# The first 560 columns of an output projection's weights come through GpSimd's queue in six loads of unequal row counts

## The chip, the core and the metric

The kernel runs on one core of a Trainium2 chip. The metric is the device time of one execution in microseconds (us); lower is better. The core has a matrix engine (TensorE, PE in the profile), a vector engine (VectorE, DVE), an activation engine (ScalarE, ACT), a general engine (GpSimd, POOL) and a synchronisation engine (SyncE, SP) that here does nothing but issue DMA transfers. The transfers of every queue are carried out by 16 DMA engines, each of which works through its own ring of packets; this text calls one of them a ring. A load is finished when all rings that had a share of it have reported.

## What is computed

One decode step of a layer with grouped-query attention over a cache, gated by a bilinear feed-forward block, for two sequences with one new token each:

```python
xn = layernorm(x)                                   # x: [2, 1, 448]
q  = xn @ wq                                        # 16 heads of 256
s  = softmax(q @ k_cache.T / 16) @ v_cache          # 8 kv heads, 4096 positions, 256 wide
s  = s @ wo                                         # wo: [4096, 448]
g  = silu((xn @ w_gate * (xn @ w_up)) @ w_down)     # inner width 1792
return x + s * g
```

All is float32. The two caches are 134 MB together, the weights the rest of some 159 MB that are read once.

## The kernel before

**Loads.** All large loads are issued by SP, in the order of `dma_side`: the gate and up weights `wgu` into the tile `low`, `wd` into `buf[1]`, `wq` into `buf[0]`, then the caches. The caches go by `N` = 16 steps (8 kv heads times 2 sequences). One transfer of 8 MB (lines 128 to 130) carries the values of step i and the keys of step i+2, 64 KB to each of the 128 partitions, into one of two buffers `buf[0]`, `buf[1]`; it is issued when the matmuls on the buffer's earlier contents are done (`sp.after(pe, "v", i - 2)`). At the end come the values of the last two steps (`vv`, line 133) and the output weights `wo` (lines 134 to 138).

**The output weights.** `wo` is laid out as 128 partitions by 32 blocks of `D` = 448 columns. It comes in six loads of 14, 9, 4, 3, 1 and 1 blocks (`ABREAST` and `DIRECT`), each with a semaphore of its own (`won`). The first three go into `low`, whose earlier contents, `wgu`, were last read some 20 us into the kernel; so they are issued directly behind `vv`, and the queue works on them as soon as it gets there. The last three go into the upper half of `buf[1]` (`late`), and wait until the matmuls on it are done.

**Compute.** PE does for each step i: `turn` (transposes of the exponentials, line 317), `scores` (keys, line 361), `values` (line 386) and `join` (line 394), with the row maxima, exponentials, sums and copies of the results on DVE and ACT. Seven rounds of a hardware loop (line 407) hold steps 0 to 13, two each. `scores(i)` waits for a copy of the query on POOL: `pool_side` ends in a loop of 16 copies (line 158), the i-th of which waits until `scores(i - 2)` is done. POOL has no other work after the first few us.

**The end.** PE goes through the six loads of `wo` in order (lines 437 to 452): a wait for the load's semaphore, and then its blocks, four matmuls to a block in the last three loads. DVE then multiplies by the gate and adds `x` (lines 295 and 298), and SP stores the result (line 140).

Of the kernel before, what the change touches and what calls it, by code (L numbers as in the profile page):

```python
# [8 lines left out]
B, D = 2, 448  # L9
# [15 lines left out]
WO = 4 * HKV  # L25
ABREAST = (14, 9, 4)
DIRECT = (3, 1, 1)


class Queue:  # L30
# [23 lines left out]
def program(nc, known, x, xo, wgu, wd, wq, kv, vv, wo, out):  # L54
    def sb(name, shape):
        return nc.alloc_sbuf_tensor(name, shape, F32).ap()

    def ps(name, shape):
        return nc.alloc_psum_tensor(name, shape, F32).ap()

    first = nc.alloc_semaphore("first")
    sems = {n: nc.alloc_semaphore(n) for n in (
        "x", "xg", "gu", "wd", "wq", "k0", "k1", "v14", "v15", "t0", "t1", "pt", "sr", "ob", "q", "m", "mx", "res")}
    won = [nc.alloc_semaphore(f"wo{i}") for i in range(len(ABREAST + DIRECT))]
    pe = Queue(nc, nc.tensor, "pe", known)
    dv = Queue(nc, nc.vector, "dv", known)
# [6 lines left out]
    low = sb("low", [128, 28 * FC])  # L73
# [5 lines left out]
    one = sb("one", [1, 1])  # L79
    xnT = sb("xnT", [128, NK, W])  # L80
    xg, gate, sig, r0, r1 = (sb(n, [128, SL]) for n in ("xg", "gate", "sig", "r0", "r1"))
    sel = sb("sel", [128, 2, 2])
    pick = sb("pick", [128, B, DUP])
    gs, hs = sb("gs", [128, 512]), sb("hs", [128, 512])
# [5 lines left out]
    m = sb("m", [128, 2])  # L90
    mx = sb("mx", [1, NT, W])
    p = sb("p", [128, 2, 512])
    su = sb("su", [128, 2])
    sr = sb("sr", [128, 128])
    r = [sb(f"r{i}i", [128, REP]) for i in range(2)]
    pT = sb("pT", [128, 2, BLK, 128])
    ob = sb("ob", [128, 512])
# [4 lines left out]
    pt = [ps(f"pt{i}", [128, NK, 128]) for i in range(2)]  # L102
# [4 lines left out]
    late = buf[1][:, ROW:]  # L107
    bounds = [0]
    for n in ABREAST + DIRECT:
        bounds.append(bounds[-1] + n)  # L110
    early = bounds[len(ABREAST)]

    def wo_step(i):
        return low[:, i * D:(i + 1) * D] if i < early else late[:, (i - early) * D:(i - early + 1) * D]

    def where(i):
        return divmod(i, B)

    def dma_side():
        e = nc.sync  # L120
        for lo, hi in zip(GU, GU[1:]):
            e.dma_start(low[:, lo:hi], wgu[:, lo:hi]).then_inc(sems["gu"], 16)
        e.dma_start(buf[1][:, :14 * D], wd).then_inc(sems["wd"], 16)
        e.dma_start(buf[0][:, :28 * 512], wq).then_inc(sems["wq"], 16)
        sp.after(pe, "y4")
        for h in range(2):
            e.dma_start(buf[1][:, h * ROW:(h + 1) * ROW], kv[0][:, h * ROW:(h + 1) * ROW]).then_inc(sems[f"k{h}"], 16)
        for i in range(N - 2):
            sp.after(pe, *(("q", 1) if i == 0 else ("s", 1) if i == 1 else ("v", i - 2)))
            e.dma_start(buf[i % 2], kv[1 + i]).then_inc(turns[i % 2], 16)  # L130
        sp.after(pe, "v", N - 4)
        for h in range(2):
            e.dma_start(buf[0][:, h * ROW:(h + 1) * ROW], vv[h]).then_inc(sems[f"v{N - 2 + h}"], 16)
        for n, lo, hi in zip(won, bounds, bounds[1:]):
            if lo == early:
                sp.after(pe, "v", N - 3)
            t = low[:, lo * D:hi * D] if hi <= early else late[:, (lo - early) * D:(hi - early) * D]
            e.dma_start(t, wo[:, lo * D:hi * D]).then_inc(n, 16)
        sp.after(dv, "res")
        e.dma_start(out, r1).then_inc(sems["res"], 16)  # L140
        e.wait_ge(sems["res"], 16)
        last = nc.alloc_semaphore("last")
        e.sem_clear(range(first.num, last.num + 1))

    def pool_side():
        e = nc.gpsimd
        po.ev(e.memset(ident, 0.0), "zero")
        po.after(po, "zero")
        po.ev(e.affine_select(out=ident, in_=ident, pattern=[[-1, 128]], compare_op=OP.not_equal, fill=1.0,
                              base=0, channel_multiplier=1), "ident")  # L150
        po.after(dv, "var")
        po.ev(e.tensor_tensor(rstd, st[:, 3:4], eh, op=OP.pow), "rstd")
        po.after(dv, "qT")
        for i in range(N):
            g, b = where(i)
            if i >= 2:
                po.after(pe, "s", i - 2)
            e.tensor_copy(qs[i % 2], qT[:, g, b, :, None, :].to_broadcast([128, 2, DUP, REP])).then_inc(sems["q"], 1)  # L158

    def act_side():  # L160
        e = nc.scalar
        e.dma_start(x2, x).then_inc(sems["x"], 16)
        ac.after(dv, "xg")
        e.dma_start(xg[0:128:DUP, :], xo).then_inc(sems["xg"], 16)
        ac.after(pe, "gu", 0)
        ac.ev(e.copy(gs[:, :FC], s[:, 0, :FC]), "g")
        ac.after(pe, "y4")
        ac.ev(e.copy(ys, o[:, :D]), "ys")
        ac.after(pe, "y")
        ac.ev(e.activation(sig, acc[:, :SL], AF.Sigmoid), "sig")  # L170
        for h in range(2):
            ac.after(pe, "q", h)
            ac.ev(e.copy(qr[h], s[:, h]), "qr", h)

        def exps(i):
            ac.after(dv, "neg", i)
            for h in range(2):
                ins = e.activation(p[:, h], s[:, h], AF.Exp, bias=m[:, 1:2], scale=1.0 / 16, accum_out=su[:, h:h + 1])  # L178
            ac.ev(ins, "exp", i)

        def half(i):
            ac.after(pe, "t", i, 1)
            e.copy(pT[:, 1], pt[1]).then_inc(sems["pt"], 1)  # L183

        exps(0)
        half(0)
        exps(1)
        for i in range(N):
            if i + 2 < N:
                exps(i + 2)  # L190
            ac.after(pe, "v", i)
            e.copy(ob, o).then_inc(sems["ob"], 1)  # L192
            if i + 1 < N:
                half(i + 1)
        ac.after(pe, "w4")
        ac.ev(e.copy(ys, o[:, :D]), "accs")
# [103 lines left out]
    def pe_side():  # L300
        e = nc.tensor
# [18 lines left out]
        def abreast(t, lhs, rhs, i, total):  # L320
            c = i % NT
            return e.matmul(t[W * c:W * (c + 1), :D], lhs, rhs, start=i < NT, stop=i >= total - NT)  # L322

        def spread(start, stop):
            for c in range(NT):
                ins = e.matmul(acc[W * c:W * (c + 1), :SL], pick.rearrange("p b j -> p (b j)"),  # L326
                               ys[:, c * SL:(c + 1) * SL], start=start, stop=stop)
            return ins
# [77 lines left out]
        at, count = dict(pe.at), pe.n  # L406
# [26 lines left out]
        def left(i):  # L433
            g, j = divmod(i, 4)
            return oT[g][:, j // 2, j % 2].rearrange("p b j -> p (b j)")

        for n, lo, hi in zip(won, bounds, bounds[1:]):
            e.wait_ge(n, 16)
            for i in range(lo, hi):
                if i >= 4 * (HKV - 1):  # L440
                    pe.after(dv, "oT", N - 1)
                if i < early:
                    ins = abreast(o, left(i), wo_step(i), i, early)
                else:
                    for c in range(NT):
                        ins = e.matmul(acc[W * c:W * (c + 1), :SL], left(i), wo_step(i)[:, c * SL:(c + 1) * SL],  # L446
                                       start=lo == early and i == lo, stop=i == WO - 1)
            if hi == early:
                pe.ev(ins, "w4")
            if lo == early:  # L450
                pe.after(ac, "accs")
                spread(False, False)
        pe.ev(ins, "fin")

    pool_side()
    act_side()
    dve_side()
    dma_side()
    pe_side()
    return {q.name: q.at for q in (pe, dv, ac, po, sp)}  # L460

# [44 lines left out]
```

## Time and profile before

| what | value |
|---|---|
| time, median of 3 runs | 374.98 us (374.97 to 375.02) |
| the profiled execution's own time | 375.17 us |
| its span, first to last instruction | 373.9 us |
| read from memory in the span | 158.54 MB, 424 GB/s |
| PE busy | 243.6 us, 65% of the span |
| DVE, ACT, POOL busy | 60.3 us, 45.7 us, 5.0 us |
| granted TensorE clock, mean | 0.794 |

The views used below are: the page's strip of the DMA engines' busy share in 40 slices; its list of DMA queues, where each row gives packets, megabytes, and the time that the packets took as a share of 16 rings' span; the chain of work that ended last; a table by stretches of time, whose last two columns are the mean busy share of the 16 rings and the rate; and the timeline of instructions. Queue q1 is SP's, q10 ACT's; "instruction" rows are the fetches of the engines' program code, which run on the same rings. In the table by stretches, a packet counts with its whole time in the stretch in which it starts, so that a share over a very short stretch is rough.

### The profile page before, as it was taken

Reading aid. Unit: us, or ns where it says so; the run is one execution under the profiler, and the core shown is the slowest. Engines: PE = TensorE matmul, PEld = TensorE weight load, DVE = VectorE, ACT = ScalarE, POOL = GpSimd, SP = SyncE. Lnnn points to the kernel's source line nnn. Section 1 sums busy time; section 2 is a strip of 40 time slices with the busy share of each in tenths; the row PEclk is TensorE's granted clock in tenths of the full one; section 3 lists DMA queues with packets and bytes.
Section 4 is the critical chain, followed back from the end, with each engine's and each line's share of the span. In section 5 each row is a group of like instructions: output and inputs, shape, how many; then the busy total and the mean of one; then the engine's idle time right before and its main releaser. Section 6 shows DMA issues by size and latency. Waiting matters only on the chain. (4 is left out here: it accounts for less than half of the span.)

```text
span 373.9 us, 3749 instructions
## 1 busy us (share of the span) xinstructions
PE 243.6 (65%) x1642; PEld 95.1 (25%) x1642; DVE 60.3 (16%) x142; ACT 45.7 (12%) x105; POOL 5.0 (1%) x23
## 2 busy tenths in 40 slices
PE   0093295739393948585776767575758484849786
PEld 0021022322322222323231313122322222232332
DVE  3001002202121212112021203030302020202100
ACT  1002021010102020202020202020202010201110
POOL 1000000000000000000000000000000000000000
PEclk9998588758677687768596859596959586958899
DMA  9999999999999999999999999999999999999995
GB/s 369 400 459 413 430 424 438 444 444 449 449 429 400 435 429 435 449 442 436 407 435 435 435 442 435 449 428 414 435 428 442 442 442 442 400 417 435 417 421 211
DMA packets 4203, 158.70 MB, mean 424 GB/s; under 512 B 610, under 2 KB 868, under 8 KB 1252
## 3 DMA queue, kind: packets, MB, share of 16 engines
q1 hardware_dynamic: 4176, 158.59, 98.4%
q8 instruction: 5, 0.08, 0.1%
q14 instruction: 2, 0.02, 0.0%
q10 hardware_dynamic: 20, 0.01, 0.0%
HBM read 158.54 MB, written 0.06 MB: 424 GB/s over the span
## 5 line engine op out<-in xcount | busy, mean ns | idle before, releaser
L361 PE MATMUL s<-buf,qs 128*32 128x512 f32 x512 | 89.2, 860 | 58.1 <-PEq L51 58.1
L386 PE MATMUL o<-buf,pT 128*32 128x512 f32 x512 | 76.9, 610 | 0.3 <-DVE oT L272 0.3
L178 ACT ACTIVATE p<-s,m 128x512 f32<-128x512 f32 x32 | 21.7, 682 | 251.6 <-DVE m L253 251.6
L361 PEld LDWEIGHTS s<-buf,qs 128*32 128x32 f32 x512 | 22.5, 151 | 111.2 <-issue 111.1
L247 DVE TENSOR_REDUCE m<-s 128x1 f32<-128x1024 f32 x16 | 19.6, 1224 | 144.8 <-PE s L361 144.8
L317 PE MATMUL pt<-ident,p 128*128 128x128 f32 x128 | 22.2, 329 | 12.8 <-PEq L51 12.8
L394 PE MATMUL oc<-sel,ob 128*128 128x2 f32 x128 | 16.4, 250 | 19.8 <-PEq L51 19.8
L386 PEld LDWEIGHTS o<-buf,pT 128*32 128x32 f32 x512 | 17.1, 111 | 32.9 <-issue 30.6
L394 PEld LDWEIGHTS oc<-sel,ob 128*128 128x128 f32 x128 | 15.5, 191 | 33.9 <-issue 33.9
L317 PEld LDWEIGHTS pt<-ident,p 128*128 128x128 f32 x128 | 17.4, 166 | 13.7 <-issue 13.7
L308 PE MATMUL s<-buf,xnT 128*32 128x512 f32 x48 | 7.9, 813 | 10.8 <-DMA buf<-wq 10.8
L308 PE MATMUL s<-low,xnT 128*32 128x448 f32 x48 | 6.5, 692 | 11.9 <-DMA low<-wgu 11.9
L266 DVE COPY pT<-pt 128x512 f32<-128x512 f32 x16 | 11.1, 691 | 18.3 <-PE o L386 17.0
L249 DVE TENSOR_REDUCE mx<-sm 1x128 f32<-1x512 f32 x16 | 10.9, 679 | 10.1 <-PE sm L367 10.1
L192 ACT COPY ob<-o 128x512 f32<-128x512 f32 x16 | 9.3, 582 | 12.5 <-PE o L386 12.5
L183 ACT COPY pT<-pt 128x512 f32<-128x512 f32 x16 | 9.6, 601 | 2.4 <-PE pt L317 2.4
L371 PEld LDWEIGHTS sm<-one,mx 1*128 1x128 f32 x32 | 4.7, 183 | 13.8 <-issue 13.8
L158 POOL COPY qs<-qT 128x64 f32<-128x64 f32 x16 | 3.7, 236 | 293.8 <-PE s L361 243.1
L377 PEld LDWEIGHTS sm<-sel,sr 128*128 128x128 f32 x32 | 7.4, 288 | 0.0
L371 PE MATMUL sm<-one,mx 1*128 1x1 f32 x32 | 6.0, 255 | 1.7 <-PEq L51 1.7
L322 PE MATMUL o<-low,oT 128*32 128x448 f32 x54 | 6.4, 544 | 0.6 <-DMA low<-wo 0.6
L178 ACT ACTIVATION_READ_ACCUMULATOR p<-s,m 128x1 f32 x32 | 6.3, 196 | 0.0
(65 smaller groups left out, 62.4 us busy)
## 6 DMA issues: line engine op xcount, KB each, us to landing
buf<-kv SPq DMA_DIRECT2D x2, 4096.0 KB, 26.1
buf<-vv SPq DMA_DIRECT2D x2, 4096.0 KB, 23.1
buf<-wq SPq DMA_DIRECT2D x1, 7168.0 KB, 41.9
low<-wgu SPq DMA_DIRECT2D x1, 5824.0 KB, 17.0
buf<-wd SPq DMA_DIRECT2D x1, 3136.0 KB, 24.0
low<-wo SPq DMA_DIRECT2D x1, 3136.0 KB, 34.8
low<-wo SPq DMA_DIRECT2D x1, 2016.0 KB, 39.1
low<-wo SPq DMA_DIRECT2D x1, 896.0 KB, 40.9
```

Of the source, the lines that this page charges most:

```text
L178: ins = e.activation(p[:, h], s[:, h], AF.Exp, bias=m[:, 1:2], scale=1.0 / 16, accum_out=su[:, h:h + 1])
L183: e.copy(pT[:, 1], pt[1]).then_inc(sems["pt"], 1)
L192: e.copy(ob, o).then_inc(sems["ob"], 1)
L247: e.tensor_reduce(m[:, 0:1], s.rearrange("p h n -> p (h n)"), axis=AX.X, op=OP.max).then_inc(sems["m"], 1)
L249: e.tensor_reduce(mx, sm[:1, None, :128].rearrange("p o (c j) -> p o j c", c=NT).to_broadcast([1, NT, W, NT]), axis=AX.X, op=OP.max).then_ ...
L266: e.tensor_copy(pT[:, 0], pt[0]).then_inc(sems["pt"], 1)
L308: e.matmul(t[W * c:W * (c + 1), :n], xnT[:, k, :], block(NT * k + c), start=k == 0, stop=False)
L317: ins = e.transpose(t[:, i, :], a[:, i * 128:(i + 1) * 128], ident)
L361: ins = e.matmul(s[W * c:W * (c + 1), h], qs[i % 2][:, d].rearrange("p j q -> p (j q)"), k[:, h, d, c, :], start=d == 0, stop=d == 1)
L371: pe.ev(e.matmul(sm[:, 128:129], mx.rearrange("p c j -> p (c j)"), one, start=True, stop=True), "x", i)
L386: ins = e.matmul(o[W * at:W * (at + 1), :], pT[:, h, j, 64 * c + 16:64 * c + 48], v[:, h, j, c, :], start=h == 0 and j < 2, stop=h == 1 an ...
L394: ins = e.matmul(oc[:, 2 * d:2 * d + 2], ob[:, h * 256 + d * 128:h * 256 + (d + 1) * 128], sel[:, h], start=h == 0, stop=h == 1)
```

## The change

Before the change each of SP's first three loads of `wo` brought all its columns. Now the first `LEAD` = 560 columns (2,240 bytes of each of the 128 partitions, 0.29 MB in all) are left out of SP's first load, and come through POOL's queue instead, early in the kernel: behind the fifth of its 16 copies (i = 4), POOL issues six loads. Five bring those columns, of 7, 34, 2, 51 and 34 rows, 128 together; between the fourth and the fifth of them stands one of a single row of 16 columns into an unused tile `skip`. The space was last read by the gate and up matmuls, so nothing has to be waited for. PE waits for the five loads (semaphore `lead`, 16 for each) before its first block of `wo`, and SP waits for the sixth (`skip`) before the store of the result.

```diff
+LEAD = D + D // 4
+SHARES = (7, 34, 2, 51, 0, 34)
...
         for n, lo, hi in zip(won, bounds, bounds[1:]):
             if lo == early:
                 sp.after(pe, "v", N - 3)
-            t = low[:, lo * D:hi * D] if hi <= early else late[:, (lo - early) * D:(hi - early) * D]
-            e.dma_start(t, wo[:, lo * D:hi * D]).then_inc(n, 16)
+            if hi <= early:
+                at = max(lo * D, LEAD)
+                e.dma_start(low[:, at:hi * D], wo[:, at:hi * D]).then_inc(n, 16)
+            else:
+                e.dma_start(late[:, (lo - early) * D:(hi - early) * D], wo[:, lo * D:hi * D]).then_inc(n, 16)
+        e.wait_ge(sems["skip"], 16)
         sp.after(dv, "res")
         e.dma_start(out, r1).then_inc(sems["res"], 16)
...
             e.tensor_copy(qs[i % 2], qT[:, g, b, :, None, :].to_broadcast([128, 2, DUP, REP])).then_inc(sems["q"], 1)
+            if i == 4:
+                row = 0
+                for n in SHARES:
+                    if n:
+                        e.dma_start(low[row:row + n, :LEAD], wo[row:row + n, :LEAD]).then_inc(sems["lead"], 16)
+                    else:
+                        e.dma_start(skip, wo[:1, :16]).then_inc(sems["skip"], 16)
+                    row += n
...
+        e.wait_ge(sems["lead"], 16 * sum(n > 0 for n in SHARES))
         for n, lo, hi in zip(won, bounds, bounds[1:]):
             e.wait_ge(n, 16)
```

On POOL, from the end of its short start to its last instruction, before the change (L158 is the copy of the query for one step):

```order
L147 MEMSET ident 128x128
L149 ISA
L149 AFFINE_SELECT ident<-ident 128x128
L152 TENSOR_TENSOR rstd<-st,eh 2x1
L158 COPY qs<-qT 128x64 x16
```

and in the changed kernel, where the copy is L165:

```order
L159 TENSOR_TENSOR rstd<-st,eh 2x1
L165 COPY qs<-qT 128x64 x5
L170 DMA low<-wo 7x560
L170 DMA low<-wo 34x560
L170 DMA low<-wo 2x560
L170 DMA low<-wo 51x560
L172 DMA skip<-wo 1x16x1
L170 DMA low<-wo 34x560
L165 COPY qs<-qT 128x64 x11
```

Six issues stand between the fifth and the sixth copy; nothing else on POOL moved. On SP, the rows from the last values to the store, before:

```order
L133 DMA buf<-vv 128x8192
L138 DMA low<-wo 128x6272
L138 DMA low<-wo 128x4032
L138 DMA low<-wo 128x1792
L138 DMA buf<-wo 128x1344 [waits pe]
L138 DMA buf<-wo 128x448 x2
L140 DMA res<-r 128x112 [waits dv]
```

and in the changed kernel:

```order
L136 DMA buf<-vv 128x8192
L142 DMA low<-wo 128x5712
L142 DMA low<-wo 128x4032
L142 DMA low<-wo 128x1792
L144 DMA buf<-wo 128x1344 [waits pe]
L144 DMA buf<-wo 128x448 x2
L147 DMA res<-r 128x112 [waits dv,skip]
```

SP's first load of `wo` is 560 columns narrower, the order of its loads is the same, and its store has one more semaphore to wait for.

More of the change, by code (lines that the diff above doesn't have):

```diff
@@ L62, in program @@
     sems = {n: nc.alloc_semaphore(n) for n in (
-        "x", "xg", "gu", "wd", "wq", "k0", "k1", "v14", "v15", "t0", "t1", "pt", "sr", "ob", "q", "m", "mx", "res")}
+        "x", "xg", "gu", "wd", "wq", "k0", "k1", "v14", "v15", "t0", "t1", "pt", "sr", "ob", "q", "m", "mx", "res", "lead", "skip")}
     won = [nc.alloc_semaphore(f"wo{i}") for i in range(len(ABREAST + DIRECT))]
@@ L81, in program @@
     xg, gate, sig, r0, r1 = (sb(n, [128, SL]) for n in ("xg", "gate", "sig", "r0", "r1"))
+    skip = sb("skip", [1, 16])
     sel = sb("sel", [128, 2, 2])
```

## The prediction

> **What bounds the kernel now.** I read the DMA strip first, then the chain that ended last, then the end by stretches, then what the rings do besides the loads. The strip and the steady middle:
>
> ```profile
> DMA  9999999999999999999999999999999999999995
> 100.00:300.00 200.00, 137.61 (x870) 53.92 (x874) 33.43 (x70) 24.07 (x60) 2.36 (x10) 0.76 1.00 432
> ```
>
> The rings are full from start to end: the last two columns say share 1.00 and 432 GB/s, which is 27.0 GB/s for each of 16 rings. PE is busy 137.61 of these 200 us and hides under them. The last pieces of the chain of waits:
>
> ```profile
> 345.57 24.41 DMA buf<-wo
> 369.97 0.04 issue
> 370.01 0.78 PE acc L446 x24
> ...
> 371.59 0.28 DVE r L295
> ```
>
> From 345.57 to 369.97 the end waits for a load of `wo`. So what counts is when the last ring finishes, and what follows it. The table by stretches shows how unevenly they finish:
>
> ```profile
> 366.00:368.80 2.80, 2.67 (x22) 0.80 (x26) 0.00 (x0) 0.00 (x0) 0.00 (x0) 1.00 0.99 393
> 368.80:370.60 1.80, 1.15 (x32) 0.59 (x28) 0.00 (x0) 0.53 (x1) 0.00 (x0) 1.00 0.33 127
> ...
> 368.80:369.00 0.20, 0.20 (x8) 0.00 (x0) 0.00 (x0) 0.00 (x0) 0.00 (x0) 1.00 0.40 152
> ...
> 369.40:369.60 0.20, 0.00 (x0) 0.00 (x0) 0.00 (x0) 0.17 (x1) 0.00 (x0) 1.00 0.43 161
> ...
> 370.00:370.20 0.20, 0.18 (x8) 0.19 (x12) 0.00 (x0) 0.00 (x0) 0.00 (x0) 1.00 0.26 99
> ...
> 370.40:370.60 0.20, 0.20 (x19) 0.20 (x12) 0.00 (x0) 0.00 (x0) 0.00 (x0) 1.00 0.12 45
> 370.60:370.80 0.20, 0.20 (x17) 0.20 (x12) 0.00 (x0) 0.00 (x0) 0.00 (x0) 1.00 0.00 0
> ```
>
> Until 368.8 all are busy. Then the share is 0.40 to 0.43, and 0.43 x 16 is 7: nine rings are done by about 368.8, seven go on. At 370.0 it is 0.26 (four), at 370.4 it is 0.12 (two), and at 370.6 nothing is left. What the seven still had to do after 368.8 is 0.33 x 16 x 1.8 = 9.5 ring-us, on average 1.4 us each, 1.8 for the last. Why seven?
>
> ```profile
> q1 hardware_dynamic: 4176, 158.59, 98.4%
> q8 instruction: 5, 0.08, 0.1%
> q14 instruction: 2, 0.02, 0.0%
> q10 hardware_dynamic: 20, 0.01, 0.0%
> ```
>
> There are seven fetches of program code inside the span. One of them, in the stretch 33.6 to 34.7:
>
> ```profile
> q8 instruction: 1, 0.02, 5.8%
> ```
>
> 5.8% of 16 x 1.1 us is 1.02 us for 16 KB, on one ring. Of a load such a ring carries the same share as the others, so the fetch makes it late to the end. Seven fetches and seven late rings: I read the lateness as theirs.
>
> **The change part by part.** *SP's first load loses 2,240 bytes in each of 128 rows*, 8 rows to a ring: 17,920 bytes at 27.0 GB/s, **0.66 us less on every ring.** The order of SP's loads stays, so this comes straight off each ring's end.
>
> *POOL's five loads bring the same bytes back, but unevenly.* How a load of few rows is divided, the only small loads of this trace show:
>
> ```profile
> x<-x ACTq DMA_DIRECT2D x1, 3.5 KB
> xg<-xo ACTq DMA_DIRECT2D x1, 3.5 KB
> ```
>
> They have 2 and 8 rows, and q10 has 20 packets: 10 rows, and 10 completions, one for each row. So each row went to a ring of its own. For POOL's queue, and for more than 16 rows, no row here shows the division. The bounds: all rows evenly (8 to a ring, nothing gained), or everything on one ring (120 rows more than its 8, x 0.083 us: 10 us lost). I take equal shares on as many rings as divide the count, at most 16, each load beginning where the last one stopped: 7 rows on 7 rings, 34 on two (17 each), 2 on two, 51 on three (17 each), and 34 on two. That is the nearest to the x rows, and gives **seven rings 17 rows and nine rings 1 row** (the load into `skip` moves 64 bytes and may shift the last two by one). 17 rows are 38,080 bytes, 1.41 us; one row is 0.08 us.
>
> *Completions and small packets.* The stretch 5.5 to 9.1 has 16 of q10's:
>
> ```profile
> q10 hardware_dynamic: 16, 0.00, 0.5%
> ```
>
> 0.5% of 16 x 3.6 us is 0.29 us, 0.02 us each. With a completion of each of six loads on each ring, that is 0.1 us a ring at most. Sum for a ring: **with one row -0.66 + 0.08 + 0.1 = -0.48 us; with 17 rows -0.66 + 1.41 + 0.1 = +0.85 us.**
>
> *What that does to the end.* If the seven late rings are among those with one row, the last of them ends 0.48 earlier, at 370.6 - 0.48 = 370.1. The early rings with 17 rows end at 368.8 + 0.85 = 369.65, still before it. That the two nearly meet says that the sizes suit each other; that the right rings are met is my assumption, since no view names the ring of a packet. Could PE be late next? Its last three waits:
>
> ```profile
> 366.13 3.23 PE L322 MATMUL o<-low,oT 128*32 128x448 f32 x26 [0.57 <-DMA low<-wo]
> 370.01 0.78 PE L446 MATMUL acc<-buf,oT 128*32 128x112 f32 x24 [0.66 <-DMA buf<-wo]
> ...
> 371.12 0.16 PEld L446 LDWEIGHTS acc<-buf,oT 128*32 128x32 f32 x8 [0.19 <-DMA buf<-wo]
> ```
>
> Each wait is for a landing, and landings that all come 0.48 earlier cut 0.48 from the first 0.57 and then move the rest along; PE follows. DVE's two steps and the store stay as they are.
>
> *POOL.* It issues six transfers behind its copy at 88.49:
>
> ```profile
> 88.49 0.24 POOL L158 COPY qs<-qT 128x64 f32<-128x64 f32 x1 [16.36 <-PE s L361]
> 108.40 0.24 POOL L158 COPY qs<-qT 128x64 f32<-128x64 f32 x1 [19.68 <-PE s L361]
> ```
>
> Queued behind them is only the copy of 108.40, 19.7 us later; that one's reader on PE, `scores(5)`, starts at 141.19 in the timeline:
>
> ```profile
> 141.19 4.39 PE L361 MATMUL s<-buf,qs 128*32 128x512 f32 x24 [3.81 <-PEq L51]
> ```
>
> An issue on SP takes 0.43 us (1.38 us for three); POOL's is not shown. Six could take 52 us (141 - 89) before PE noticed; the lower bound is nothing. I take nothing. If a software queue were that slow, each us beyond it would be a us of the run.
>
> *The two waits.* PE's for `lead` stands in front of a matmul that starts at 362.36, some 250 us after the loads; even if each of a ring's 17 rows let one 64 KB packet (65,536 bytes at 27.0 GB/s, 2.4 us) pass first, they are through by 89 + 41 + a few us. SP's for `skip` stands in front of its wait for the result, and nothing else is queued. Both 0. In the middle, the heavy rings run 1.4 us late for a while, no more than those that met a fetch; the queue always has work, so nothing stalls.
>
> Sum: **-0.48 us**, bounds -0.66 (a ring with no row and no completions) and, on the wrong side, +0.85 to +10. The profiled execution's 375.17 would become 374.7; it stands 0.19 above the median, so the median goes from 374.98 to **374.50**.
>
> **Rivals.** *(1) The bytes are charged where they arrive.* All of the 27.0 GB/s of a ring may be the limit of the 8 partitions that it fills, not of the ring. Then a row that another ring brings still costs the late ring's partitions 0.083 us, the late rings gain nothing, and the heavy rings, which write against a busy ring, take up to 2 x 1.41 us for their rows: 368.8 - 0.66 + 2.8 = 370.9, 0.3 behind the present end. Time 374.9 to 375.4, say 375.2. For it: the rate is the same 432 GB/s throughout, as a fixed port would have it. Against, weakly: the fetches cost a ring time although they go to no tile. The Trainium skill, "SBUF — State Buffer", Door 1, gives this form: 16 ports of 27.2 GB/s chosen by partition; the trace's 27.0 agrees, and cannot tell the port from the ring. 0.20.
>
> *(2) Slower: 17 rows fall on one of the last two rings.* Seven of 16 rings are heavy. If one of the two that are still busy at 370.4 is among them, the end comes 0.85 later: 375.8. It decides as soon as one late ring is heavy: from rings that end after 370.6 - 0.85 = 369.75 on, that is five, a heavy one is behind the present end. For it: the `skip` load may or may not move the last share by a ring. 0.17.
>
> *(3) The change doesn't do what it says:* POOL's queue cuts every load into 16 nearly equal parts, and each ring gets about 8 rows again, the first ones up to 12: +0.1 to +0.4, 375.1. The Trainium skill, "DMA: Bandwidth & Descriptors", "Why a DMA increments its semaphore by 16 and not by 1", has both: the largest divisor up to 16 as the rule, and as an exception measured on some direct copies from GpSimd sixteen parts of rounded-up size. By the rule the time is my forecast, by the exception this rival's; no run here shows either yet. 0.12.
>
> *(4) An eighth fetch.* POOL and PE have a few instructions more. A fetch on a late ring costs the 1.02 us above or more: 376. 0.06.
>
> **Numbers.** Forecast 0.40 (374.4 to 374.65), and 0.05 for more than it, where a fetch falls away and the late rings are fewer: up to 1 us, 374.0. 0.2% is 0.75 us, about what a measurement can tell from no change; the forecast is inside it. Over 0.75 faster: only the last 0.05. Slower by over 0.75: most of (2) (0.13), (4) (0.06) and a tail of (1) (0.01), 0.20. Within: 0.75. Range 374.3 to 375.8: it leaves out the rare gain and the tail of (2) and (4).
>
> **What would show it.** In the changed profile a POOL queue with about 128 rows plus completions behind 88 us; still seven instruction fetches; the DMA share near 0.9 or more until 369.5 and then down to 0 by 370.1 (right), or 0.4 from 368.5 on with an end past 370.6 (rings met wrongly), or the old staircase (even division). An end of the DMA past 371 while the fetches stay seven would make the prediction wrong.

## The result, and the profile after

| | before | changed |
|---|---|---|
| median | 374.98 us (5 runs, 374.96 to 375.04) | 377.30 us (5 runs, 376.95 to 377.53) |
| profiled execution, its own time | 375.17 us | 377.53 us |
| its span | 373.9 us | 376.2 us |

The changed kernel is slower: 1.0061 times the time of before, 95% interval 1.0046 to 1.0076, which is +2.3 us. The forecast was -0.48 us. The profiled execution is the slowest of its five.

The list of DMA queues of the changed kernel, first (columns as before):

```profile
q1 hardware_dynamic: 4176, 158.30, 98.1%
q0 software_dynamic: 240, 0.29, 0.2%
q8 instruction: 5, 0.08, 0.1%
q10 hardware_dynamic: 20, 0.01, 0.0%
q14 instruction: 2, 0.02, 0.0%
```

There are seven fetches of program code as before, SP's queue carries 0.29 MB less, and POOL's queue (q0) carries it. Its packets take 0.2% of the time of 16 rings, 0.2% x 376 = 0.75 us on a ring, about what SP's queue was spared; taken alone, nothing here is 2.3 us long. The end by stretches:

```profile
366.00:368.80 2.80, 2.22 (x24) 0.55 (x20) 0.00 (x0) 0.00 (x0) 0.00 (x0) 1.00 0.96 397
368.80:370.60 1.80, 1.80 (x18) 0.48 (x10) 0.00 (x0) 0.00 (x0) 0.00 (x0) 1.00 0.95 373
370.60:372.40 1.80, 1.17 (x13) 0.26 (x16) 0.00 (x0) 0.53 (x1) 0.00 (x0) 1.00 0.34 132
372.40:373.00 0.60, 0.60 (x28) 0.60 (x32) 0.00 (x0) 0.00 (x0) 0.00 (x0) 1.00 0.05 21
```

The staircase of before is still there, as tall as it was: full until 370.6, then 0.34 for 1.8 us (0.33 before), and one last ring beyond it (0.05 x 16 is 0.8). It only stands some 2 us later. So all rings are late, not only some; the change neither levelled the rings nor overloaded a few. The chain of waits says when the loss had happened:

```profile
347.96 24.34 DMA buf<-wo
```

SP issued the last loads at 347.96 instead of 345.57, and from there everything is as before: the 2.4 us were lost earlier. Where, the table by stretches shows for the 40 us in which POOL's loads run, first before, then in the changed kernel, with a later stretch of the changed kernel behind it:

```profile
90.00:130.00 40.00, 27.79 (x173) 11.09 (x171) 6.69 (x14) 4.82 (x12) 0.47 (x2) 0.74 1.01 435
```

```profile
90.00:130.00 40.00, 25.39 (x166) 9.68 (x162) 5.94 (x14) 4.82 (x12) 2.96 (x7) 0.74 1.01 419
180.00:300.00 120.00, 81.03 (x518) 32.46 (x522) 20.08 (x42) 14.47 (x36) 1.43 (x6) 0.76 1.00 432
```

The rings are busy throughout in both (1.01), but move 419 GB/s in place of 435; after that they are back at 432. 16 GB/s for 40 us are 0.64 MB, more than twice the 0.29 MB that POOL's loads carry, and these are counted in the 419. (A packet of 64 KB counts where it starts, so such a rate is good to some 1%.) POOL itself is not the cause:

```profile
89.46 2.24 POOL L170 DMA_DIRECT2D low<-wo  x4
91.69 0.52 POOL L172 DMA_DIRECT2D skip<-wo  x1
92.20 0.53 POOL L170 DMA_DIRECT2D low<-wo  x1
109.52 0.24 POOL L165 COPY qs<-qT 128x64 f32<-128x64 f32 x1 [16.80 <-PE s L376]
```

The six issues take 3.3 us, 0.55 each, and POOL then waits 16.80 us for PE.

**The rings one by one.** The trace has the start, duration and size of each packet, but not its ring. In this trace a ring works without a gap, and SP's packets come in the same order of sizes on each; so the packets can be strung into 16 sequences, each packet behind the one that ended just before it. Rings only a few ns apart can be confused, and behind 365 us, among many short packets, they often are; the figures below are good to some 0.1 us. The eight rings that carry the eight rows of `xg` (one each) are the first eight. As a measure I take the time in which a ring does the first five 8 MB loads, 40 packets of 64 KB, from about 61 to 158 us, and the median over rings that meet no fetch in it:

```
us for five loads      first eight   other eight
before                    96.74         96.74
changed                   99.40         98.92
six_tiny                  96.90         96.88
skip_only                 96.74         96.76
one_even                  97.48         97.51
act_even                  97.50         97.50
two_halves                99.64         99.57
act_halves                99.55         99.57
halves_280                98.01         98.01
eighths                   99.79         99.81
own_ports                 97.49         96.82
crossed                   98.77         98.20
dst_crossed               98.74         98.07
src_crossed               97.51         96.83
```

(The kernels below "changed" are the experiments.) The rings that do meet a 16 KB fetch in this time need 98.3 us before, 1.6 more than the others: that bears out the prediction's reading that the late rings are those with a fetch. In the changed kernel POOL's 128 rows are spread over 13 rings, mostly 8 to 12 on one; three rings have none. And these three need 98.3 to 98.4 us, with no fetch: **a ring that moves no row of the new loads loses 1.6 us while they run.** A 64 KB packet takes 2.42 us; many of those that run beside the new packets take 2.6 to 2.9 us, on rings with rows and without.

### The profile page after: what moved, and what is told of

Its sections match the earlier page's. It is cut to its first block, busy times and chain, and to the rows that moved or that the text cites. A ratio compares the mean times of both kernels' runs of the same rounds, so it can differ in the third digit from the quotient of the medians.

```text
span 376.2 us, 3757 instructions
## 1 busy us (share of the span) xinstructions
PE 244.1 (65%) x1642; PEld 95.0 (25%) x1642; DVE 60.4 (16%) x142; ACT 45.8 (12%) x105; POOL 8.2 (2%) x29
## 5 line engine op out<-in xcount | busy, mean ns | idle before, releaser
L165 POOL COPY qs<-qT 128x64 f32<-128x64 f32 x16 | 3.7, 238 | 292.8 <-PE s L376 243.2
```

## The experiments

Each was run beside the kernel before on the same chip, in three groups: six_tiny to act_even, two_halves to crossed, and the last four. The medians of before in these were 375.06, 375.02 and 375.08 us. The code cuts leave out the semaphores; the waits are moved to where each kernel's loads need them. In six_tiny, skip_only and the four kernels with 64 rows SP's loads of `wo` are whole, as before the change. Three theories stood at the start: each load on POOL's queue has a price on every ring; the rows themselves cost, by bytes or by packets; and the program starts worse with such a queue (in the changed kernel's profiled run one ring began its third load's packets at 18.38 us, the latest of before at 17.83).

**six_tiny: the same six loads, 64 bytes a row, SP's loads whole.**

```diff
-e.dma_start(low[row:row + n, :LEAD], wo[row:row + n, :LEAD])
+e.dma_start(tiny[row:row + n, :], wo[row:row + n, :16])
```

> SP's loads as before the change; POOL issues its six loads at the same place with the same row counts, but of 16 columns (64 bytes a row) into a spare tile. Price-per-load theory (each load on POOL's queue delays every ring, whatever it carries; six cost the 1.5 us that the changed kernel's rings without a row lost): 1.3 to 2.0 us over before, 376.3 to 377.0. Bytes theory (the loss is the bytes of the unevenly divided rows): at most 0.1 over, 375.1. Start theory (a program with loads on POOL's queue starts worse): like the changed kernel's start, one ring about 1 us late before 18 us.

375.21 us, ratio 1.0004 (0.9994 to 1.0014). The rings lose 0.15 us. The theory of a price for each load, which asked for 376.3 to 377.0, falls: six loads with all their completions are nearly free.

**skip_only: the load of 64 bytes alone.**

```diff
-for n in SHARES: ...
+e.dma_start(skip, wo[:1, :16])
```

> SP's loads as before the change; POOL issues the one load of 64 bytes alone. Price-per-load theory: a sixth of the six, 0.2 to 0.4 us over before, 375.2 to 375.4. Bytes theory: 375.0. Start theory: as much late as with six, 0.5 to 1 us over.

375.17 us, 1.0004 (0.9995 to 1.0014), and 0.02 us on a ring. The load into `skip` costs nothing that can be measured. The start theory falls with these two as a rule for programs with such a queue: both have POOL's queue, and their latest ring begins its third load at 17.81 and 17.89 us.

**one_even: the same columns in one load of 128 rows.**

```diff
-for n in SHARES: ...
+e.dma_start(low[:, :LEAD], wo[:, :LEAD])
```

> The 560 columns come through POOL's queue in one load of 128 rows, 8 to a ring. Price-per-load theory: the bytes cancel and one load's price is left, 375.2 to 375.4. Bytes theory (the uneven division was all that hurt): 375.0 to 375.1. A price for each row (a row's packet lengthens the large packet behind it by 0.2 to 0.4 us): eight rows on each ring, 1.0 to 2.5 us over, 376 to 377.5.

375.17 us, 1.0002 (0.9992 to 1.0011). Each ring moves 8 rows and is 0.75 us later in the middle, 0.094 us a row, and SP's narrower load gives it back at the end. The bytes of the change, on its queue and at its time, cost no more than the scatter when they come in one load of 128 rows; a price for each row's packet, which asked for 376 to 377.5, falls too. The rate in the stretch that fell to 419 in the changed kernel:

```profile
90.00:130.00 40.00, 26.98 (x172) 11.19 (x170) 6.69 (x14) 4.82 (x12) 0.47 (x2) 0.74 1.03 442
```

**act_even: the same load from ACT's queue.**

```diff
+            if i == 2:
+                e.dma_start(low[:, :LEAD], wo[:, :LEAD])
```

> The same single load of 128 rows by 560 columns, at about the same time, from ACT's queue. If the price belongs to POOL's software queue: 375.0 to 375.1. If it belongs to any second queue that mixes small packets between large ones: what the load on POOL's queue costs, within 0.2 us.

375.15 us, 1.0004 (0.9995 to 1.0014): as from POOL. Its packets run later than expected, at 136 to 156 us instead of 93 to 103 from POOL; the price is the same.

So neither the queue, nor the number of loads, nor the bytes alone. What was left is an assumption on the division: in one load of 128 rows a ring fills the same 8 partitions as in SP's loads of 128 rows. In loads of 34 or 51 rows it fills others, those that another ring is just filling with its 64 KB packets (below: foreign partitions). No view names a ring or its partitions; the next experiments test this **destination theory** by its effect.

**two_halves and eighths: one_even cut into loads of 64 and of 16 rows.**

```diff
-e.dma_start(low[:, :LEAD], wo[:, :LEAD])
+for row in range(0, 128, 64):
+    e.dma_start(low[row:row + 64, :LEAD], wo[row:row + 64, :LEAD])
```

In eighths both 64 are 16.

> The 560 columns come through POOL's queue in two loads of 64 rows, so each ring again moves 8 rows, but half of them into rows that another ring fills in all of SP's loads. Destination theory (a row costs more where its destination is not the one that its ring fills in SP's loads; the changed kernel's 26 us of ring time beyond the bytes, over some 115 such rows, is 0.22 us each): 64 such rows, 14 us of ring time, 0.9 us on a ring, 376.0. Count theory (only the number of rows on a ring counts): as with one load of 128 rows, 375.2.

> The same in eight loads of 16 rows: each ring moves 8 rows, nearly all of them into rows that other rings fill. Destination theory: some 120 such rows, 1.6 us on a ring, 376.7 to 377.2. Count theory: 375.2 to 375.3 (two more completions than with six loads).

377.40 us, 1.0063 (1.0046 to 1.0080), and 377.33 us, 1.0065 (1.0048 to 1.0081). Still 8 rows on each ring, still the same bytes; one load cut in two costs all that the change costs. The count theory falls. The destination theory has the direction, but my size for two_halves was wrong (376.0), and that for eighths a little low (376.7 to 377.2): half the rows in foreign partitions cost nearly as much as almost all of them, 2.1 and 2.3 us more on a ring than one_even. The rate fell as in the changed kernel:

```profile
90.00:130.00 40.00, 24.81 (x162) 10.09 (x162) 5.86 (x14) 4.82 (x12) 0.82 (x3) 0.74 1.03 419
```

**own_ports and crossed: the same rows by the same rings, to their own partitions or to others.** SP's loads are whole; 64 rows come in addition.

```diff
+for c in range(4):
+    for h in range(0, 64, 32):
+        at = 0 + h + c
+        e.dma_start(low[at:at + 29:4, :LEAD], wo[at:at + 29:4, :LEAD])
```

In crossed the 0 is 64. SP's load of these columns comes some 200 us later and writes the same space; SP first waits for the eight loads, which have long landed.

> SP's loads as before the change (whole). POOL brings 64 rows of 560 columns in addition, in eight loads of 8 rows into partitions c, c+4 to c+28 (c = 0 to 3 and 32 to 35) of the space that SP's load overwrites at the end; if a load of 8 rows is one row on each of the first eight rings, every row goes where its ring's rows go in SP's loads. Both theories: the first eight rings 0.7 to 0.8 us later, the others as before; 375.1 to 375.9.

> As own_ports, but into partitions 64 higher: the same rings, the same number of rows and bytes, into the rows that the other eight rings fill. Destination theory: the first eight rings lose 1.5 us or more, and the other eight, which move none of it, lose 0.7 us or more; 376.0 to 377.0. Count theory: as own_ports, within 0.2 us, and the other eight rings lose nothing.

375.48 us, 1.0010 (1.0001 to 1.0020), against 376.78 us, 1.0045 (1.0028 to 1.0062). In own_ports the first eight rings lose 0.75 us, their 8 rows at 0.094, and the other eight 0.08. In crossed the first eight lose 2.03, and the other eight, which move nothing, 1.46. That this is one row of each load on each of the first eight rings is seen too: of own_ports' 16 sequences six carry 8 of the new rows, six carry none, and the other four, which the stringing confuses, share the last 16.

**dst_crossed and src_crossed: only the destination, or only the source, 64 rows higher.**

```diff
-e.dma_start(low[at:at + 29:4, :LEAD], wo[at:at + 29:4, :LEAD])
+e.dma_start(low[at + 64:at + 93:4, :LEAD], wo[at:at + 29:4, :LEAD])     # dst_crossed
+e.dma_start(low[at:at + 29:4, :LEAD], wo[at + 64:at + 93:4, :LEAD])     # src_crossed
```

> As crossed, but only the destinations are 64 partitions higher; what is read are the rows of own_ports (its columns are overwritten by SP's whole load at the end, so the output is the reference's). Destination theory: as crossed, 376.5 to 377.0, the eight rings without a row 1.4 us late in the middle. Source theory (it is reading other rows of wo that costs): as own_ports, 375.0 to 375.8.

> The reverse: destinations as in own_ports, what is read are the rows 64 higher. Destination theory: as own_ports, 375.0 to 375.8. Source theory: as crossed, 376.5 to 377.0.

376.83 us, 1.0044 (1.0028 to 1.0061), against 375.63 us, 1.0012 (1.0002 to 1.0021). It is the destination: the rings of dst_crossed are those of crossed within 0.13 us, those of src_crossed those of own_ports within 0.02. This also bears out the assumption on the division: where the edits send a ring's rows to the partitions taken for its own, a row costs 0.094 us, as in one_even. The queue's row and the rate, of dst_crossed and then of own_ports:

```profile
q0 software_dynamic: 256, 0.14, 0.1%
...
90.00:130.00 40.00, 26.81 (x170) 10.02 (x167) 5.97 (x14) 4.82 (x12) 4.00 (x9) 0.74 1.00 419
```

```profile
q0 software_dynamic: 256, 0.14, 0.1%
...
90.00:130.00 40.00, 27.23 (x172) 10.74 (x170) 6.69 (x14) 4.82 (x12) 3.35 (x8) 0.74 1.02 440
```

The same 256 packets with the same bytes; 419 or 440 GB/s by where they are put.

**act_halves: two_halves from ACT's queue.**

```diff
-    e.dma_start(low[:, :LEAD], wo[:, :LEAD])
+    for row in range(0, 128, 64):
+        e.dma_start(low[row:row + 64, :LEAD], wo[row:row + 64, :LEAD])
```

> two_halves from ACT's queue. If POOL's software queue has a part in the price: between 375.2 and 376.5. If it is the destinations alone: as two_halves, 377.1 to 377.5.

377.05 us, 1.0057 (1.0041 to 1.0074), 0.05 below the range for destinations alone, and 99.55 and 99.57 us on the rings against 99.64 and 99.57. So POOL's queue has no part in it that shows here. ACT's packets run at 137 to 161 us, and there the rate falls in act_halves (first), and does not in act_even:

```profile
135.00:165.00 30.00, 16.38 (x107) 6.84 (x111) 3.84 (x10) 2.41 (x6) 0.24 (x1) 0.69 1.01 403
```

```profile
135.00:165.00 30.00, 18.80 (x115) 8.08 (x119) 3.52 (x8) 2.41 (x6) 0.24 (x1) 0.68 1.01 434
```

**halves_280: two_halves with half the columns.**

```diff
-LEAD = D + D // 4
+LEAD = 280
```

> two_halves with half the columns, 1,120 bytes a row instead of 2,240. If the price goes by bytes (a ring and a destination share a rate while both write): half of two_halves' 2.4 us, 376.1 to 376.4. If it goes by rows or packets: as two_halves less nothing, 377.0 to 377.4.

376.02 us, 1.0027 (1.0015 to 1.0038): +0.94 where two_halves has +2.38. On a ring it is 1.27 us for 8 rows of 1,120 bytes, against 2.87 for 8 of 2,240. The number of rows is the same, so a price for each row alone falls. It goes nearly by bytes, though the 0.94 is a little under half (the range was 376.1 to 376.4); six_tiny, with 64 bytes a row and hardly a loss, fits that.

No kernel here beats the one before. dst_crossed speaks against relieving a late ring through others: eight rows that other rings bring cost the ring whose partitions receive them 1.33 us (98.07 - 96.74), and eight that it brings itself 0.75.

## Why the prediction was wrong

*What bounds the kernel*: right. The rings decide, the late ones are, as far as the strung rings show, those with a fetch (1.6 us for one of 16 KB in the five loads of before), and the tail after the last landing did not change.

*-0.66 us on each ring by SP's narrower load*: right. one_even loses 0.75 in the middle and ends 0.11 us above before; 0.75 - 0.66 is 0.09.

*Completions and small packets, 0.1 us*: right; six_tiny shows 0.15.

*POOL's issues and the two waits, nothing*: right. 3.3 us of issuing behind the fifth copy, and POOL still waits for PE; the loads landed some 235 us before PE asked for them (about 128 and 364 us).

*"Equal shares on as many rings as divide the count ... seven rings 17 rows and nine rings 1 row"*: **wrong**. The rows went to 13 rings, in sixteen parts of rounded-up size: at most 3 rows on a ring of the loads of 34, and 4 of the load of 51, so up to 12 on one ring. The sizes of POOL's packets show it without any stringing: 47 carry two rows and 34 one row, just what these parts give if two rows share a packet; 17 rows on a ring would give 56 and 16. I had taken equal shares from two loads of 2 and 8 rows, in which both rules give the same. The rounded-up parts are the exception that the Trainium skill's "DMA: Bandwidth & Descriptors", "Why a DMA increments its semaphore by 16 and not by 1", states for some direct copies from GpSimd; the trace agrees with it. They were rival 3, to which I had given 0.12. By itself it would have been a small miss: for a late ring with 11 rows, 11 x 0.094 + 0.15 - 0.66 is +0.5 us, 375.5. This is an estimate; no kernel here divides the rows unevenly into own partitions.

*The sum for a ring, bytes and 0.1 us*: **wrong, and the larger part of the miss.** It lacks the term for the destination: it put at nothing what a row costs when it goes into partitions that another ring is filling. The rings without a row lost 1.6 us, where the sum gives 0.1; over all rings that meet no fetch the five loads took 99.0 us on average, 2.3 above before, of which 8 rows are 0.75 and the rest, 1.55 us, is for the destinations. At the end SP's narrower load takes off 0.66, which leaves 2.25 - 0.66 = 1.6 us for the late ring that met its fetch at 363.3; the last ring but one did end 1.59 later (372.25 against 370.65 for the last of before). The very last ring ended 0.7 later still, at 372.96. One ring's first large packet took 2.79 us instead of 1.72, 85 us ahead of POOL's loads, and a ring that late with a fetch would end about there. No other trace here has such a start. Without it the profiled execution would come to 376.8; but the other four executions, of which there is no trace, took 376.95 to 377.41. So 1.6 of the 2.3 us are accounted for; in the profiled execution the rest may be that late ring, and what it is in the other four stays open.

*Rival 1* had the mechanism (bytes are charged where they arrive), and I gave it 0.20, but mis-sized it at 375.2: I let the receiving ring lose the time of the bytes, 0.083 us a row, and the moving one at most twice that. By its figures eight foreign rows cost the receiving ring 0.66 us and the moving one at most 1.33; measured in dst_crossed they cost 1.33 and 2.00. Why both lose more than a shared rate gives is open; so is why 64 foreign rows in two_halves, where every ring gives and takes, cost nearly as much as 120 in eighths.

*Rivals 2 and 4*: no ring got 17 rows, and there was no eighth fetch.

## What to carry to other kernels

A small load beside a stream that fills all rings cost little more than its bytes here (0.094 us a row, 0.083 by the rate) where each ring fills the partitions that it fills in the stream, and some four times its bytes where it doesn't (2.87 us for 8 rows in two_halves), on rings that carry none of it too. So send side loads over all 128 partitions, or check that the split matches. To even out rings by giving some of them other rings' rows did not pay on this stream: the receiver lost more than if it had moved the rows itself. And before a load of an odd row count is used to aim at certain rings, its split has to be looked at in a trace: small counts don't tell one rule from another.

## What the runs showed of the hardware that was not expected

- A row of 2,240 bytes costs a ring 0.094 us in its own partitions. Eight rows in another ring's partitions cost 2.00 us on the ring that moves them and 1.33 us on the ring that usually fills them (dst_crossed, from GpSimd's queue). The two loads of 64 rows cost the same from GpSimd's queue (99.6 us for five loads in two_halves) and from ACT's (99.6 in act_halves).
- The rings show as fully busy meanwhile (share 1.00 to 1.03 in the stretches in which the rate falls to 419 GB/s, or 403): here the busy share does not show this loss, the rate does.
- Loads of 64-byte rows next to the stream cost a ring 0.02 to 0.03 us each, completions included, and an issue on POOL took 0.51 to 0.68 us in the changed kernel.
